# A new written order for the steps of a linear-attention and feed-forward kernel, with the epsilon constants and the bias made early

## The chip, the cores and the metric

The kernel runs on one core of one Trainium2 chip. A core has five engines that work side by side, each through its own list of instructions in order: the matmul engine (PE), the vector engine (DVE), the activation engine (ACT), GpSimd (POOL) and SyncE (SP), which here only issues transfers. Work is handed from one to another by semaphores. The metric is the device time of one execution in microseconds (us); lower is better.

## What is computed

x is 2048 tokens by 448 values, bfloat16. It is normalised, and the output is x + A(xn) + B(xn):

```
xn  = (x - mean) / sqrt(var + 1e-5)
A:  q, k, v = split(xn @ wqkv)              16 heads of 28
    pq, pk  = q @ w_phi, k @ w_phi          per head
    phi     = [softmax(p), softmax(-p)]     56 features
    kv = phi_k^T v,  z = sum_s phi_k
    A  = ((phi_q kv) / (phi_q z + 1e-6)) @ wo
B:  h = xn @ w1 + b1                        1792 features
    B = (h * tanh(softplus(h))) @ w2
```

## The kernel before

The tokens are taken as 16 tiles of 128 (t), in 8 pairs (u). The whole program is a list of named steps. The string ORDER (lines 147 to 161) gives the sequence in which they are recorded, and each engine executes its own instructions in that sequence; each instruction waits only for what it reads or for a place that it overwrites (`Program.op`, L53, and `resolve`, L89). So ORDER decides three things: what each engine does next, in which order SyncE's queue issues the transfers, and which pair of the eight PSUM banks a step gets (`take2`, L391: the pair of banks longest unused).

The steps that the change and the prediction speak of:

- `lx0s` to `lx6s`: loads of x by SyncE (L270); `lx1s` has tiles 2 and 3, `lx2s` 4 and 5, `lx3s` 6 and 7, `lx0s` 0 and 1, `lx4s` 8 to 11, `lx6s` 12 to 15. `lkms lkts lvms` load the weights of k and v, `lqT0` to `lqT3` those of q by transposing transfers (L285), `l1m0s` to `l1m2s` and `l1ts` w1, `l2s` w2, `los` wo, `lbs` the bias (L302), `lpa` w_phi.
- `pi` makes the identity on POOL (L320), `pp pw pm pv pk` other constants; `pk` is mask2 and the zeros of KVT (L349). `ep` is three small instructions on DVE (L362 to L368) that add up columns of the identity into epsT, the epsilon of the denominator. `b1` transposes the bias on PE (L688) and copies it out of PSUM on DVE (`bias_T`, L686).
- `st4d` is the statistics of tile 4 on DVE (L458 and L459), `st5a` the same on ACT (L450 to L454). `rs4p` is 1/sqrt of pair 4 on POOL (L464, L467), `rs4a` and `rs3t` on ACT (L471, L473; `t` tile by tile). `xn4d` normalises pair 4 on DVE in three instructions (L492); `xn7p` does it on POOL (L487), behind a small DVE instruction `sh7` (L480). `xt1d`, `xt1b` transpose the pair on PE and evacuate it on DVE or on both; `xt4m` does it by a transposing transfer of SyncE (L512, called `xTm4` below).
- `wtk0b wmk0b wmq1d bd` and the like fold w_phi into the weights of k and q (L533 to L593); `qd` copies a piece of WqT on DVE. `wmq0`, `wmq1` make Wpq.
- `k1F k1H`, and likewise q and v: pair 1 times the weights, in a part F (three full chunks of 128 rows, six matmuls) and a part H (the last 64 rows, two matmuls side by side); `pair_part` (L418) opens a pair of banks with the first of the two parts and evacuates with the second. `exk`, `exq` are the exponentials on ACT (L614, L675), `ve1` the evacuation of v on ACT or DVE (L507; the letter at the end of the part that comes second says which).
- `kn1.0` sums E of pair 1 (L622) and takes the reciprocal (L624) on DVE, and multiplies on POOL (L626). `kv0` to `kv7` multiply with v on PE (L643), `kvz` masks the sum and adds epsT on DVE (L655), and sends it through a transposing transfer to KVZ.
- `e5` turns the exponentials of q by a transposing transfer (L683, `eT5`). `nd5` is numerator and denominator of tile 5 on PE (L717) and the division on DVE (L732 to L743), `ot2m` turns pair 2 (L752). `f0.3F`, `f0.3H`: chunk 3 of 14 of the feed-forward for half 0 of the tokens on PE, with Mish on ACT (L694). `g5` is the second feed-forward matmul (L818), `wo2F wo2H` the projection (L834); `finish` adds x on DVE (L783). `sto`, `stt` store.

A `kn` step, the place where DVE hands its work to POOL (L622 to L627):

```
        op("DVE", lambda e: e.tensor_reduce(Sk[u][:, s, :], Eh(), AX.X, ALU.add), r=[("E", u, s)], w=[("Sk", u, s)],
           tag=f"Sk{u}.{s}")
        op("DVE", lambda e: e.reciprocal(rSk[u][:, s, :], Sk[u][:, s, :]), r=[("Sk", u, s)], w=[("rSk", u, s)],
           tag=f"rSk{u}.{s}")
        op("POOL", lambda e: e.tensor_tensor(Eh(), Eh(), ap_on(rSk[u][:, s, 0:1], [[1, 2 * H], [0, DH]]), ALU.mult),
           r=[("E", u, s), ("rSk", u, s)], w=[("E", u, s)], tag=f"phik{u}.{s}")
```

Of the kernel before, what the change touches and what calls it, by code (L numbers as in the profile page):

```python
# [144 lines left out]


ORDER = """
lpa lx1s pi lx3s lkms lkts lvms table lx2s st3d pp pw pm lqT1 st6d st2a pv st7d z16 rs3t rs1a xn3d xn1d lqT2 lqT3 lqT0
wtk0b bd xt3b wtk1b xt1d wmk0b st4d v3Fd wmk1d st5a lx6s qd rs2t xn2d lx0s v1Fd v1Ha v3Ha st15d st14d rs7p k1F wmq1d
st12d xn7p wmq0a lx4s st10d xt2m k3F st9d st8d rs4p st11d rs5p st13d k1H l1ts k3H xn4d xt7m q3H q1H q1F l1m2s rs6p q3F  # L150
xn5d xn6p q2F k2F kn3.0 xt4m v2Fd v2Hd xt5m q2H st0d st1d k2H xt6m v7Ha v7Fa rs0p k7F k4F k7H l1m1s e3 xn0d k4H xt0m
v5Hd k6H lbs pk kn1.1 kn3.1 k6F v5Fd kn7.0 kn6.1 k5F k0F k5H e6 kn5.0 v6Ha q4H kn2.0 e2 k0H q4F l1m0s e7 v6Fd ep q6F
v0Fd b1 v0Hd q6H f1.3H f0.0H f1.3F e8 f1.1F f0.0F kn5.1 kn7.1 kn0.1 v4Fa e9 v4Ha kn1.0 f1.0H e13 e12 f1.1H f0.1H kn4.1
kn4.0 f1.0F f0.1F f1.2F los q7H kn6.0 q5H kn0.0 f1.2H q0H e5 e4 kn2.1 q7F q5F q0F f1.13F kv5 kv0 kv7 kv4 kv3 kv6 kv1
kv2 f0.13H f1.13H f0.12H f0.12F f0.13F e0 kvz wob f0.3F e1 f1.8H f0.3H f0.11H l2s nd0 f1.8F f0.11F f1.10F nd1 f1.10H
ot0m e10 e14 e11 f1.9H nd2 f1.9F f1.12F f0.8F f1.12H f0.7H f0.8H nd3 f0.7F f0.2F f1.7F nd5 e15 f1.7H f1.11H f0.2H
f1.11F f0.9F nd4 f1.4H f0.10H f0.9H f1.4F f0.10F ot1m ot2m f0.6F f0.4H f0.5H f0.6H nd12 f0.5F f0.4F f1.5F nd13 f1.6H
ot6m nd8 f1.5H f1.6F g0 g1 wo6F nd7 wo0H nd9 wo6H g12 g13 ot4m wo2F wo0F g5 wo2H nd6 ot3m nd10 nd11 g4 g8 g7 g9 wo3H
ot5m nd15 nd14 wo4H ot7m g6 wo4F g14 g2 g3 g11 wo1F wo7F wo5F wo1H wo5H wo7H sto1 wo3F g10 sto6 sto0 sto5 sto3 sto4
g15 stt14 sto2 stt15  # L160
"""


# [806 lines left out]
```

## Time and profile before

| | us |
|---|---|
| median of 3 runs | 156.01 (155.85 to 156.04) |
| profiled execution | 155.94 |
| its span, first to last instruction | 154.2 |
| PE busy in it | 148.2 |
| DVE, ACT, POOL busy | 103.4, 74.2, 40.9 |

A row of a timeline has the start in us from the span's beginning, the length in us (of a merged group of rows the length from first start to last end), the engine (PE, DVE, ACT, POOL; SPq is SyncE's issue of transfers), the line of the kernel, the operation, what is written from what, the shape (for PE rows*columns of the array, then the moving block), the count, and in brackets the idle time of the engine just ahead of it and what ended that. A row of a table of groups has the same names, then total busy us and mean ns of one, then idle us and releasers. A row of transfers ends with KB each and us from issue to landing.

### The profile page before, as it was taken

To read this page: it belongs to the slowest core of one execution; us is meant where nothing else is said; L and a number is where in the kernel's file an instruction comes from. 1 tells how busy PE (TensorE), PEld (TensorE's weight loads), DVE (VectorE), ACT (ScalarE), POOL (GpSimd) and SP (SyncE) were. 2 spreads that over 40 slices of the span, in tenths; PEclk is the share of its full clock that TensorE was granted. 3 is DMA by queue.
4 is the path that set the end of the run, shared out by engine and by line. 5 is a ranking of instruction groups with operands and counts; after the bars stand their busy time and mean duration, and the time that the engine had idled before them with its cause. 6 is when DMAs were issued, how large, how long until landed. Compare 5 with 4: busy or idle time off the path is not lost.

```text
span 154.2 us, 2908 instructions
## 1 busy us (share of the span) xinstructions
PE 148.2 (96%) x1185; PEld 73.1 (47%) x1185; DVE 103.4 (67%) x228; ACT 74.2 (48%) x94; POOL 40.9 (27%) x58
## 2 busy tenths in 40 slices
PE   7999898999799999999999999999999999999992
PEld 2475343445244457444444444555555555555451
DVE  0897999799999803077978576849759879400641
ACT  3898979889498799676547766100000000000000
POOL 7300679799589991000000000000000000000000
PEclk9999999999999999999999999999999999999999
DMA  5987779998799103994986110300302030300057
GB/s 133 283 135 292 155 154 204 244 173 182 132 168 275 44 6 66 142 286 130 97 169 129 30 34 0 60 4 2 60 0 48 16 60 0 60 4 0 26 194 256
DMA packets 39993, 17.17 MB, mean 111 GB/s; under 512 B 33964, under 2 KB 39212, under 8 KB 39980
## 3 DMA queue, kind: packets, MB, share of 16 engines
q1 hardware_dynamic: 39372, 16.87, 49.4%
q8 instruction: 9, 0.15, 0.4%
q10 hardware_dynamic: 608, 0.12, 0.4%
q14 instruction: 4, 0.03, 0.1%
HBM read 7.02 MB, written 1.84 MB: 57 GB/s over the span
## 4 chain that ended last, share of the span: by engine, by line
PE 71%; DVE 14%; SPq 5%; DMA 3%; POOL 3%; issue 2%; DVEq 0%; POOLq 0%
PE PS L430 32%; PE PS L818 27%; PE PS L834 7%; DVE Sk L622 4%; SPq L285 3%; DVE stats L458 3%; PE PS L717 3%; DMA x_all<-in_A_x_dram 3%; PE PS L643 2%; POOL rstd L467 2%; DVE v_all L507 2%; DVE rSk L624 1%; DVE mv L459 1%; SPq L270 1%; SPq L281 1%
## 5 line engine op out<-in xcount | busy, mean ns | idle before, releaser
L430 PE MATMUL PS<-xnT,W 128*128 128x512 bf16 (+1 forms) x224 | 45.8, 379 | 1.0 <-DVE b1T L507 1.0
L818 PE MATMUL PS<-W,actT 128*128 128x448 bf16 (+1 forms) x224 | 43.2, 351 | 0.0
L694 ACT ACTIVATE actT<-PS,b1T 128x1024 bf16<-128x1024 f32 x28 | 30.8, 1114 | 13.6 <-PE PS L430 13.2
L818 PEld LDWEIGHTS PS<-W,actT 128*128 128x128 bf16 x224 | 21.7, 98 | 20.1 <-issue 0.4
L430 PEld LDWEIGHTS PS<-xnT,W 128*128 128x128 bf16 (+1 forms) x224 | 17.8, 97 | 23.7 <-issue 2.6
L626 POOL TENSOR_TENSOR actT<-actT,rSk 128x896 bf16<-128x896 bf16 x16 | 26.7, 1698 | 3.2 <-DVE rSk L624 3.2
L783 DVE TENSOR_TENSOR x_all<-PS,x_all 128x448 bf16<-128x448 f32 (+1 forms) x16 | 9.2, 614 | 16.8 <-PE PS L834 14.2
L622 DVE TENSOR_REDUCE Sk<-actT 128x32 f32<-128x896 bf16 x16 | 16.6, 1039 | 0.0
L614 ACT ACTIVATE actT<-PS 128x896 bf16<-128x896 f32 x16 | 13.4, 927 | 1.7 <-PE PS L430 1.7
L732 DVE COPY Sq<-PS 128x16 f32<-128x16 f32 x32 | 4.0, 168 | 13.8 <-PE PS L717 13.8
L430 PE MATMUL PS<-Wkv,xnT 128*128 128x448 bf16 (+1 forms) x64 | 12.8, 353 | 0.0
L430 PE MATMUL PS<-Wpk,xnT 128*128 128x448 bf16 (+1 forms) x64 | 12.4, 353 | 0.4 <-DVE v_all L507 0.4
L430 PE MATMUL PS<-Wpq,xnT 128*128 128x448 bf16 (+1 forms) x64 | 12.1, 353 | 0.5 <-DVE Wpq L507 0.5
L458 DVE BATCH_NORM_STATS2 stats<-x_all 128x6 f32<-128x448 bf16 x14 | 8.5, 608 | 4.7 <-DMA x_all<-in_A_x_dram 4.7
L743 DVE TENSOR_TENSOR xn<-v_all,rden 128x448 bf16<-128x448 f32 x16 | 10.0, 625 | 1.8 <-DMA Wkv<-xn 0.7
L740 DVE TENSOR_TENSOR v_all<-v_all 128x464 f32<-128x464 f32 x16 | 10.3, 642 | 0.6
L736 DVE TENSOR_TENSOR v_all<-PS,Sq 128x464 f32<-128x464 f32 x16 | 10.3, 641 | 0.5
L738 DVE TENSOR_TENSOR v_all<-PS,Sq 128x464 f32<-128x464 f32 x16 | 10.1, 631 | 0.0
L675 ACT ACTIVATE actT<-PS 128x896 bf16<-128x896 f32 x10 | 8.6, 933 | 1.0 <-PE PS L430 1.0
L430 PEld LDWEIGHTS PS<-Wpq,xnT 128*128 128x128 bf16 (+1 forms) x64 | 5.1, 97 | 6.6 <-issue 1.1
L430 PEld LDWEIGHTS PS<-Wpk,xnT 128*128 128x128 bf16 (+1 forms) x64 | 5.0, 97 | 6.8 <-issue 1.8
L430 PEld LDWEIGHTS PS<-Wkv,xnT 128*128 128x128 bf16 (+1 forms) x64 | 5.2, 97 | 5.6 <-issue 1.5
(85 smaller groups left out, 122.3 us busy)
## 6 DMA issues: line engine op xcount, KB each, us to landing
W<-in_B_w_dram SPq DMA_DIRECT2D x1, 1568.0 KB, 7.4
out_dram<-x_all SPq DMA_DIRECT2D x7, 224.0 KB, 2.2
W<-in_B_w_dram SPq DMA_DIRECT2D x3, 448.0 KB, 4.1
x_all<-in_A_x_dram SPq DMA_DIRECT2D x4, 224.0 KB, 3.6
x_all<-in_A_x_dram SPq DMA_DIRECT2D x2, 448.0 KB, 4.3
Wkv<-in_A_wqkv_dram SPq DMA_DIRECT2D x2, 336.0 KB, 4.7
Wo<-in_A_wo_dram SPq DMA_DIRECT2D x2, 336.0 KB, 4.3
W<-in_B_w_dram SPq DMA_DIRECT2D x2, 224.0 KB, 3.5
```

What stands on the lines that cost most here:

```text
L430: ins = e.matmul(o, lhs(c, k), rhs(c, k), start=first and c in (0, 3), stop=not first and c in (2, 3))
L458: op("DVE", lambda e: e.bn_stats(stats[:, t, :], x_all[:, t, :]), r=[("x", t)], w=[("st", t)], tag=f"bn{t}")
L614: op("ACT", lambda e, s=s: e.activation(E_of(u)[:, s, :, :], two(b, D), ACT.Exp, scale=1.0 if s == 0 else -1.0), r=[pb(b), pb(b + 1)], w=[ ...
L622: op("DVE", lambda e: e.tensor_reduce(Sk[u][:, s, :], Eh(), AX.X, ALU.add), r=[("E", u, s)], w=[("Sk", u, s)], tag=f"Sk{u}.{s}")
L626: op("POOL", lambda e: e.tensor_tensor(Eh(), Eh(), ap_on(rSk[u][:, s, 0:1], [[1, 2 * H], [0, DH]]), ALU.mult), r=[("E", u, s), ("rSk", u, ...
L694: op("ACT", lambda e: e.activation(actT[:, fc, q * 1024:(q + 1) * 1024], bank(b, 2), ACT.Mish, bias=b1T[:, fc:fc + 1]), r=[("b1T",), pb(b) ...
L736: op("DVE", lambda e: e.tensor_tensor(tv(t1[i]), num(0), sx(1), ALU.mult), r=[pb(b), pb(b + 1), ("Sq", i, 1)], w=[("t1", i)], tag=f"ta{t}")
L738: op("DVE", lambda e: e.tensor_tensor(tv(t2), num(1), sx(0), ALU.mult), r=[pb(b), pb(b + 1), ("Sq", i, 0)], w=[("t2",)], tag=f"tb{t}")
L740: op("DVE", lambda e: e.tensor_tensor(t1[i], t1[i], t2, ALU.add), r=[("t1", i), ("t2",)], w=[("t1", i)], tag=f"tc{t}")
L743: op("DVE", lambda e: e.tensor_tensor(o_sb[(t // 2) % 2][:, t % 2, :].rearrange("p (h d) -> p h d", d=DH), t1[i][:, :, 0:DH], ap_on(rden[i ...
L818: ins = e.matmul(bank(b)[:, 0:width(t)], actT[:, fc, tok(t)], W2[:, fc, 0:width(t)], start=first and fc == 0, stop=last and fc == FC - 1)
L834: ins = e.matmul(bank(b)[:, 0:n], oT_of(u)[lo:hi, cc * P:(cc + 1) * P], Wo[lo:hi, cc, 0:n], start=first and c in (0, 3), stop=last and c i ...
```

## The change

It replaces the string ORDER by another with the same 290 steps in a new sequence. Fifteen of them go to another engine or form. `ep` comes third, behind `pp` and `pi`, and so is the first work of DVE; before, it stood in the middle. `lbs` comes behind `lvms` in SyncE's queue, and `b1` ahead of `v3Fa` on PE; before, `lbs` stood behind `xt0m`, and `b1` behind the matmuls of v0F. `lqT2` now stands ahead of `lx2s`. `pk` is made at the start instead of behind `rs0p`. The other forms: `rs0` from POOL to ACT, `rs3` from ACT to POOL, `rs4 rs5` from POOL to ACT, `st5` from ACT to DVE, `xt1` from DVE alone to both, `wmk1` from DVE to ACT, `wmq0` from ACT to DVE and `wmq1` from DVE to ACT, and the evacuation of v4 from ACT to DVE and of v0 from DVE to ACT (of v1, v3, v6 and v7 only the letter of the part that comes first changes, which evacuates nothing). No function changes.

```diff
@@ -145,19 +145,19 @@
 
 
 ORDER = """
-lpa lx1s pi lx3s lkms lkts lvms table lx2s st3d pp pw pm lqT1 st6d st2a pv st7d z16 rs3t rs1a xn3d xn1d lqT2 lqT3 lqT0
-wtk0b bd xt3b wtk1b xt1d wmk0b st4d v3Fd wmk1d st5a lx6s qd rs2t xn2d lx0s v1Fd v1Ha v3Ha st15d st14d rs7p k1F wmq1d
-st12d xn7p wmq0a lx4s st10d xt2m k3F st9d st8d rs4p st11d rs5p st13d k1H l1ts k3H xn4d xt7m q3H q1H q1F l1m2s rs6p q3F
-xn5d xn6p q2F k2F kn3.0 xt4m v2Fd v2Hd xt5m q2H st0d st1d k2H xt6m v7Ha v7Fa rs0p k7F k4F k7H l1m1s e3 xn0d k4H xt0m
-v5Hd k6H lbs pk kn1.1 kn3.1 k6F v5Fd kn7.0 kn6.1 k5F k0F k5H e6 kn5.0 v6Ha q4H kn2.0 e2 k0H q4F l1m0s e7 v6Fd ep q6F
-v0Fd b1 v0Hd q6H f1.3H f0.0H f1.3F e8 f1.1F f0.0F kn5.1 kn7.1 kn0.1 v4Fa e9 v4Ha kn1.0 f1.0H e13 e12 f1.1H f0.1H kn4.1
-kn4.0 f1.0F f0.1F f1.2F los q7H kn6.0 q5H kn0.0 f1.2H q0H e5 e4 kn2.1 q7F q5F q0F f1.13F kv5 kv0 kv7 kv4 kv3 kv6 kv1
-kv2 f0.13H f1.13H f0.12H f0.12F f0.13F e0 kvz wob f0.3F e1 f1.8H f0.3H f0.11H l2s nd0 f1.8F f0.11F f1.10F nd1 f1.10H
-ot0m e10 e14 e11 f1.9H nd2 f1.9F f1.12F f0.8F f1.12H f0.7H f0.8H nd3 f0.7F f0.2F f1.7F nd5 e15 f1.7H f1.11H f0.2H
-f1.11F f0.9F nd4 f1.4H f0.10H f0.9H f1.4F f0.10F ot1m ot2m f0.6F f0.4H f0.5H f0.6H nd12 f0.5F f0.4F f1.5F nd13 f1.6H
-ot6m nd8 f1.5H f1.6F g0 g1 wo6F nd7 wo0H nd9 wo6H g12 g13 ot4m wo2F wo0F g5 wo2H nd6 ot3m nd10 nd11 g4 g8 g7 g9 wo3H
-ot5m nd15 nd14 wo4H ot7m g6 wo4F g14 g2 g3 g11 wo1F wo7F wo5F wo1H wo5H wo7H sto1 wo3F g10 sto6 sto0 sto5 sto3 sto4
-g15 stt14 sto2 stt15
+pp pi ep lpa pk lx1s st3d table lx3s st2a lkms z16 pw pm st6d lkts lvms st7d rs1a lbs lqT2 lx2s rs3p pv xn1d xn3d
+wtk0b bd xt1b wtk1b xt3b wmk0b st5d wmk1a st4d v1Fa v1Ha rs2t lqT1 k3H v3Ha lqT3 lqT0 qd lx6s b1 xn2d lx0s lx4s v3Fa
+wmq1a xt2m st14d wmq0d st15d l1m2s k3F rs7p l1m1s st12d xn7p k1F q1H k1H q1F q3F k2F st9d st8d v2Hd st13d rs4a xt7m
+k2H e2 rs6p xn4d xn6p q2H q3H st11d st0d st10d v2Fd kn1.1 q2F k7F xt4m st1d rs5a v7Fd xn5d xt6m kn2.1 e7 v4Ha rs0t e3
+q4H v7Ha xn0d k7H v4Fd kn2.0 q4F k4F q6F e6 kn7.1 kn3.0 xt5m xt0m l1m0s v6Hd q6H k4H k6H v6Fd kn7.0 e13 k6F k0F k5F
+v0Hd e12 l1ts k5H kn4.1 kn1.0 k0H kn6.0 v5Hd v0Fa v5Fd q0F f1.1F q0H kn3.1 f1.1H f0.2H e5 f1.0H f1.0F kn0.1 kn6.1
+kn5.1 los f0.2F f0.3F f0.1F e8 e9 e1 f0.1H q5H f0.3H e4 q7H kn5.0 q5F q7F f0.11F kv5 kv6 kv7 kn0.0 kn4.0 kv2 e0 kv3
+kv1 kv0 kv4 e11 e14 f0.11H f1.2H kvz f0.8H f0.8F f1.2F e15 f1.11F f0.6F nd2 f0.6H f1.11H f0.9H f0.9F f0.12F nd0 f1.12H
+f0.12H e10 nd1 f1.12F f0.7F f1.7F f1.7H f1.10H f0.7H nd3 f1.10F ot0m l2s f1.3F f1.13F nd5 f1.13H f0.5H f1.3H f0.5F
+f1.4F ot1m nd4 f0.13H f1.4H nd6 f0.13F f1.6F f0.4F f1.6H f0.10H f0.4H nd7 f0.10F f1.8F ot3m f0.0F nd10 f1.8H f0.0H
+f1.5H f1.5F ot2m f1.9F wo1F nd13 f1.9H nd11 wo1H g2 g7 g3 g1 wo3F ot5m wo3H nd12 wo0H nd14 g6 wo0F wo2F g0 g5 ot6m nd8
+nd9 wo2H nd15 g4 g11 wo5F g8 sto2 ot7m ot4m g13 g9 g12 sto1 g10 wo7F wo6F wo4F wob wo5H wo7H wo6H wo4H sto3 sto5 g14
+sto6 g15 sto4 stt14 sto0 stt15
 """
```

## Prediction

> **What bounds the kernel now.** I read the page's shares first, then the timeline of the matmul engine for the places where it waits, then the timelines of the engines it waits for, then the issues of SyncE.
>
> ```profile
> span 154.2 us, 2908 instructions
> ...
> PE 148.2 (96%) x1185; PEld 73.1 (47%) x1185; DVE 103.4 (67%) x228; ACT 74.2 (48%) x94; POOL 40.9 (27%) x58
> ...
> 16.46 4.06 PE L430 MATMUL PS<-Wpq,xnT 64*128 64x448 bf16 x22 [0.54 <-DVE Wpq L507]
> 25.31 2.93 PE L430 MATMUL PS<-Wpk,xnT 128*128 128x448 bf16 x16 [0.41 <-DVE v_all L507]
> 40.69 4.38 PE L430 MATMUL PS<-xnT,W 64*128 64x512 bf16 x20 [1.03 <-DVE b1T L507]
> 56.77 3.33 PE L643 MATMUL PS<-actT,v_all 128*60 128x112 bf16 x128
> 60.03 5.57 PE L430 MATMUL PS<-xnT,W 64*128 64x512 bf16 x30
> ```
>
> PE is busy for 148.2 of 154.2 us; between its warm-up and the output it waits at three places: 0.54 + 0.41 + 1.03 = 1.98 us. The change alters the order of PE's work and hardly its amount, so about 2 us can be won at most, and new waits can cost more. Behind kv (L643, 56.77 to 60.03) PE never waits, so the two orders are told apart in the first 60 us.
>
> **The wait of 1.03 us.**
>
> ```profile
> 38.89 1.66 DVE L367 SCALAR_TENSOR_TENSOR epsT<-epsT 128x1 f32<-128x1 f32 x1
> ...
> 38.84 1.70 POOL L626 TENSOR_TENSOR actT<-actT,rSk 128x896 bf16<-128x896 bf16 x1
> ```
>
> One element took DVE 1.66 us: L367 starts 0.05 us behind a product of 1.70 us on POOL and ends with it (40.55 against 40.54). The reductions, reciprocals and PSUM reads of DVE run beside such products at their usual length, so it is this kind of instruction that waits for POOL. The bias stands behind it on DVE, and a bank that PE wants behind the bias. With `ep` first on DVE and `b1` early, this pair stands between PE and no bank: 1.03 us go. `ep` itself now runs when the identity is made, on POOL behind the three memsets of `pp`, while DVE otherwise waits for the first x; it costs nothing.
>
> **The start, to 16 us.**
>
> ```profile
> 4.07 0.48 SPq L270 DMA_DIRECT2D x_all<-in_A_x_dram  x1
> 4.59 5.11 SPq L285 DMA_TRANSPOSE WqT<-in_A_wqkv_dram  x4
> 9.74 1.53 SPq L270 DMA_DIRECT2D x_all<-in_A_x_dram  x3
> ...
> 30.06 0.61 SPq L302 DMA_DIRECT2D b_rows<-in_B_b_dram  x1
> ...
> x_all<-in_A_x_dram SPq DMA_DIRECT2D x1, 448.0 KB, 4.0
> ...
> 13.79 0.63 DVE L458 BATCH_NORM_STATS2 stats<-x_all 128x6 f32<-128x448 bf16 x1 [1.00 <-DMA x_all<-in_A_x_dram]
> 15.28 1.12 DVE L507 CAST Wpq<-PS 128x448 bf16<-128x448 f32 x2
> ```
>
> `lbs` (0.61) now goes ahead of `lx2s`, all of `lqT` and `lx6s lx0s lx4s`. `lx6s` is issued at 9.74 + 0.61 = 10.35 and lands 4.0 later, at 14.4 (before: 13.75, and DVE waited for it). `lx2s` falls behind one of the transposes as well (1.28 by pitch), to about 6.0; DVE has until 14.4 for its two tiles. DVE then takes one tile's statistics (0.73, below), not two, between that landing and the evacuation of Wpq: 14.4 + 0.73 + 1.12 = 16.25. PE's `q1H` starts at 16.3, where `q3H` started at 16.46; PE has done `b1` more and `k1H` (0.18) less. So the 0.54 us wait stays, in effect: I take 0. POOL now makes `pk`, `vare3`, `rstd3` and `pv` ahead of `bd`, so Wbd and `wmk0b` come some 0.5 us later; that lies inside the same wait of PE, and would cost its 0.5 without it.
>
> **DVE from 14.4 to the first `kn`.**
>
> ```profile
> 18.59 0.59 DVE L458 BATCH_NORM_STATS2 stats<-x_all 128x6 f32<-128x448 bf16 x1
> ...
> 19.32 0.59 DVE L458 BATCH_NORM_STATS2 stats<-x_all 128x6 f32<-128x448 bf16 x1
> ...
> 28.68 1.07 DVE L622 TENSOR_REDUCE Sk<-actT 128x32 f32<-128x896 bf16 x1
> 29.79 0.35 DVE L624 RECIPROCAL rSk<-Sk 128x32 f32<-128x32 f32 x1
> ...
> 37.70 1.03 DVE L507 CAST v_all<-PS 128x896 bf16<-128x896 f32 x1
> ...
> 19.80 0.71 POOL L467 TENSOR_TENSOR rstd<-lnv,mhalf 128x2 f32<-128x2 f32 x1
> ```
>
> A tile's statistics have a pitch of 0.73. Nine of them make 6.57; `wmq0d` 1.05, `sh7` with its wait for POOL's rstd7 (0.71) 0.5, `xn4d` 0.9, `sh6` 0.15, `ve2` 0.95, `Sk1.1` and `rSk1.1` 1.45: 14.4 + 11.6 = 26.0, say 26.1. Before, `xn5d` came ahead of every `kn`, and `xn0d` when POOL had no product in hand. Now `xn5d` follows `kn1.1` with one tile's statistics between, and `xn0d` follows `kn2.1` directly. Each `kn` leaves 1.70 us of product on POOL. Whether xn's L492 waits for a product as L367 did, the trace shows over no product. From both sides: nothing, or the rest of the product, for each. The nearest rows:
>
> ```profile
> 21.26 0.37 DVE L492 TENSOR_SCALAR xn<-x_all,mv,rstd 128x384 bf16<-128x384 bf16 x1
> 21.71 0.63 DVE L492 TENSOR_SCALAR xn<-x_all,mv,rstd 128x448 bf16<-128x448 bf16 x2
> 21.47 0.25 POOL L464 TENSOR_SCALAR lnv<-mv 128x2 f32<-128x2 f32 x1
> ...
> L492 DVE TENSOR_SCALAR xn<-x_all,mv,rstd 128x448 bf16<-128x448 bf16 x6 | 2.3, 388 | 1.2 <-POOL rstd L467 1.1
> ...
> L492 DVE TENSOR_SCALAR xn<-x_all,mv,rstd 128x64 bf16<-128x64 bf16 x6 | 1.8, 296 | 0.3 <-ACT rstd L473 0.3
> ```
>
> On DVE an instruction starts about 0.08 before the last one's record ends, so the one at 21.71 was due at 21.55; it starts as POOL's short one ends (21.72). POOL got in between two such instructions, and DVE waited. Also, 384 more elements cost L492 92 ns, about 4 per ns, where L622 takes 1.07 us for 896: it is another kind of access than the reduction's. So I take the upper end. The Trainium skill, page "SBUF — State Buffer", section "Who interferes with whom", says that GpSimd and VectorE share a pair of ports as an exclusive lock held for a whole instruction, and that a VectorE instruction needs it when it has two SBUF inputs or runs in a two-port mode, which `tensor_scalar` can. L367 (two SBUF inputs, 1.66 us) agrees, and by that rule L492 waits too: 157.0 as forecast; if only two-input instructions waited, it would be the second rival's 155.0.
>
> With the waits: the product of `kn1.1` runs from 26.2 to 27.9. `xn5d`, due at 26.8, waits 1.1 and ends at 28.8; `kn2.1` is through DVE at 30.2. The first of `xn0d`'s three instructions is ahead of POOL (0.39), then POOL's waiting product goes, 30.5 to 32.2, and the other two end at 32.8, 1.7 late. `ve4` behind them ends at 33.8. Without the waits it would end at 31.0.
>
> **PE in the same stretch.**
>
> ```profile
> 20.36 1.30 PE L430 MATMUL PS<-Wpk,xnT 128*128 128x448 bf16 x6
> 21.49 1.59 PE L430 MATMUL PS<-Wkv,xnT 128*128 128x448 bf16 x8
> 22.92 0.35 PE L430 MATMUL PS<-Wpq,xnT 64*128 64x448 bf16 x2
> ...
> 65.76 4.06 PE L430 MATMUL PS<-xnT,W 128*128 128x512 bf16 x18
> ...
> 70.73 4.81 PE L430 MATMUL PS<-xnT,W 128*128 128x512 bf16 x24
> ...
> 17.30 1.74 POOL L487 TENSOR_SCALAR xn<-x_all,rstd,shift 128x448 bf16<-128x448 bf16 x3 [0.83 <-DVE shift L480]
> ...
> 26.52 0.95 ACT L505 ACTIVATE v_all<-PS 128x896 bf16<-128x896 f32 x1
> ...
> xnT<-xn SPq DMA_TRANSPOSE x1, 3.3
> ```
>
> From start to start an F part of q, k or v takes 1.13 to 1.14, F with H 1.43, an H alone 0.18 to 0.19 (0.35 with the pipeline's tail): so 0.1 for each change to H. Of the feed-forward, three F take 4.06, 1.35 each, and three F with three H 4.81, 0.25 for an H. From 16.3 these bring PE to `k7F` at 23.4; `xTm7` is issued at about 20.0, behind POOL's `xn7p` (1.74, from `sh7` at 18.2), and lands at 23.3 to 23.8 (two W1 loads now go before it). `k4F` needs the banks of v7: ACT's `ln0` waits for `st1d` on DVE (26.9), then `ve7` (0.95) ends at 28.4. Three F later, at 31.9, `v6H` takes the banks that held v4 and needs `ve4`: 33.9. So PE stands for 2.0 us. From `v6H` to `kv5` lie nine F at 1.14, eleven H at 0.19, six F at 1.35, five H at 0.25 and five changes: 22.2; the same rates fall about 0.5% short of the stretch from 16.46 to 56.77, its waits taken out, so 22.3. `kv5` starts at 56.2, and after kv's 3.26 the next step at 59.45.
>
> POOL does not set a later time:
>
> ```profile
> 43.09 14.95 POOL L626 TENSOR_TENSOR actT<-actT,rSk 128x896 bf16<-128x896 bf16 x9 [2.55 <-DVE rSk L624]
> ```
>
> That is 1.66 each; the fourteen products behind `rSk2.0` (35.2) end at 58.5, and `kv4`, the last eighth of kv, at 58.9.
>
> **The sum.** Before, kv ended at 60.03 with one more feed-forward step done (1.35 + 0.25): 58.45 for the same work. Now 59.45: +1.0 us. The waits of 1.98 become 0.5 at `q1H`, some 0.5 to 1 around `k7F` and `k4F`, and 2.0 at `v6H`. Behind kv the order costs nothing as long as `nd2` finds KVZ:
>
> ```profile
> 60.15 1.38 DVE L655 SCALAR_TENSOR_TENSOR KVT<-PS,epsT,mask 60x448 bf16<-60x448 f32 x2 [6.48 <-PE PS L643]
> ...
> KVZ<-KVT SPq DMA_TRANSPOSE x1, 3.2
> EqT<-Eq SPq DMA_TRANSPOSE x1, 4.7
> ```
>
> KVZ lands 1.5 + 3.2 = 4.7 behind kv, at 64.2, under four F and three H of feed-forward (6.2 us, to 65.6); with the longest flight of a transpose seen (4.7) it would land at 65.7, so this cover is 1.4 us thick and each further us would count. The profiled execution took 155.94 (1.74 around its span), 0.07 below the median of 156.01; on the median's scale the forecast is 157.0, with its own range 156.3 to 157.7 from the landing of `lx6s`, which moves DVE and PE alike (0.6 either way).
>
> **Rivals.**
> - DVE keeps its turn through all of `xn0d`, and POOL's product waits 0.9 instead. For: DVE is ahead by some 0.2 us. Against: POOL got in at 21.72. `ve4` ends at 32.1, 0.2 after `v6H` is due, and kv ends at 57.7: 155.25. Chance 0.18.
> - L492 doesn't wait for POOL, only the two-input L367 does. `ve4` (31.0) is in time, kv ends at 57.45: 1.0 us faster, 155.0. Chance 0.14.
> - All three waits go and none comes: 154.0. Against: `lx6s` is issued later, not earlier. Chance 0.05.
> - The late DVE of the forecast drags SyncE's queue: `xTm0`, behind `xn0d` (32.8), lands with a flight of 4.7 at 37.6, 0.5 after `k0F` is due, and W1's tail, issued behind `eT13 eT12` and so behind q6's exponentials, is late by as much again in front of `f1.1F`. It decides from a flight of 4.2 us on; 157.6, or 158.2 with `lx6s` late too. Chance 0.13.
>
> **How the numbers follow.** The forecast has 0.5. A measurement of this kernel tells 0.2% (0.3 us) from no change. Slower: the forecast and the last rival but for the forecast's lowest edge, 0.60. Faster: the first three rivals but for an edge of the first, 0.33. Within 0.2%: 0.07. The range goes from 154.9, just below the second rival, to 158.2.
>
> **What would show it.** L492 records of over 1 us at about 27 and 30, ending with a product of POOL; a wait of PE of about 2 us between 32 and 34, put down to DVE's v_all L507; L367 at 0.2 us or less before the first statistics; no wait of PE for b1T; kv from about 56 on. It is wrong if L492 keeps 0.3 to 0.4 us beside a product, if PE's wait for v4's banks is under 0.8 us, or if PE waits behind kv.

## The result, and the profile after

| | median us | lowest to highest | runs | ratio to before, 95% |
|---|---|---|---|---|
| before | 155.97 | 155.85 to 156.04 | 4 | |
| after | 157.12 | 156.81 to 157.42 | 4 | 1.0074 (1.0049 to 1.0099) |

The new order is 1.15 us slower. The profiled execution of after took 156.91 us, that of before 155.94. These are the page's first lines and then the matmul engine's timeline of after, the rows that answer to those of before:

```profile
span 154.6 us, 2902 instructions
...
PE 148.8 (96%) x1185; PEld 73.8 (48%) x1185; DVE 104.7 (68%) x229; ACT 73.8 (48%) x95; POOL 38.8 (25%) x54
```

```profile
16.51 0.36 PE L430 MATMUL PS<-Wpq,xnT 64*128 64x448 bf16 x2
...
26.38 0.36 PE L430 MATMUL PS<-Wkv,xnT 64*128 64x448 bf16 x2 [0.30 <-DMA xnT<-xn]
...
33.38 0.36 PE L430 MATMUL PS<-Wkv,xnT 64*128 64x448 bf16 x2 [1.42 <-DVE v_all L507]
...
43.72 1.46 PE L430 MATMUL PS<-xnT,W 128*128 128x512 bf16 x6 [0.39 <-ACT v_all L505]
...
55.92 3.34 PE L643 MATMUL PS<-actT,v_all 128*60 128x112 bf16 x128
59.19 6.11 PE L430 MATMUL PS<-xnT,W 64*128 64x512 bf16 x30
65.52 0.40 PE L717 MATMUL PS<-KVZ,EqT 56*128 56x60 bf16 x16 [0.22 <-DMA KVZ<-KVT]
```

The three waits of before (0.54, 0.41, 1.03; 1.98 us) are gone, and four others have come: 0.30 at `v4H` for pair 4's transposed xn, 1.42 at `v6H` for the evacuation of v4, 0.39 at `f1.1F`, 0.22 for KVZ; 2.33 us. The step behind kv starts at 59.19; the same work was done at 58.45 before, so kv is 0.74 late. The arithmetic closes if the start is counted in: before, PE had work up to 15.92 and then waited 0.54; in after it is busy up to 16.51 with hardly more work, 0.59 late. 0.59 + 0.30 + 1.42 + 0.39 - 1.98 = 0.72. These terms don't stand for themselves, though: `v6H` starts when DVE has evacuated v4, so a PE that came there earlier would only wait longer (in `a_dma` below the 0.30 is gone, and the wait at `v6H` is 1.72). With KVZ's 0.22 the last group of matmuls is 0.95 late, as the two timelines show, first before, then after:

```profile
150.61 0.57 PE L800 MATMUL PS<-W,actT 128*128 128x64 bf16 x14
```

```profile
151.56 0.57 PE L800 MATMUL PS<-W,actT 128*128 128x64 bf16 x14
```

The spans differ by only 0.4 us, because the last store landed in 1.7 us in after's profile and in 2.3 in before's; the time outside the span was 2.3 against 1.7. For a comparison the last matmul or the whole time is the better mark.

Where the 1.42 comes from shows in DVE's and POOL's timelines of after (the rows at 30.14, 30.35 and 31.95 are the parts of one group, `xn0d`, in time order):

```profile
27.05 1.79 DVE L492 TENSOR_SCALAR xn<-x_all,mv,rstd 128x448 bf16<-128x448 bf16 x3
...
30.14 0.30 DVE L492 TENSOR_SCALAR xn<-x_all,mv,rstd 128x448 bf16<-128x448 bf16 x1
30.35 1.68 DVE L492 TENSOR_SCALAR xn<-x_all,mv,rstd 128x64 bf16<-128x64 bf16 x1
31.95 0.37 DVE L492 TENSOR_SCALAR xn<-x_all,mv,rstd 128x384 bf16<-128x384 bf16 x1
32.24 1.08 DVE L507 CAST v_all<-PS 128x896 bf16<-128x896 f32 x1
```

```profile
26.51 1.70 POOL L626 TENSOR_TENSOR actT<-actT,rSk 128x896 bf16<-128x896 bf16 x1 [2.80 <-DVE rSk L624]
30.30 1.70 POOL L626 TENSOR_TENSOR actT<-actT,rSk 128x896 bf16<-128x896 bf16 x1 [2.09 <-DVE rSk L624]
```

Three L492 take some 0.9 us alone. `xn5d` took 1.79, `xn0d` 2.18, so they lost 0.9 and 1.3. In `xn5d` the first of the three has a record of 1.29 us, to 28.34, where POOL's product ended at 28.21. In `xn0d` the first instruction gets through, POOL's product starts at 30.30, and the second, 64 elements wide, has a record of 1.68 us that ends with the product (32.03 against 32.00). That is a wait, though the profile's page counts it as busy. `ve4` ends at 33.32, and `v6H` starts 0.06 later.

The two small steps, in DVE's timeline of after:

```profile
2.77 0.16 DVE L367 SCALAR_TENSOR_TENSOR epsT<-epsT 128x1 f32<-128x1 f32 x1
...
12.39 0.17 DVE L507 CAST b1T<-PS 128x14 f32<-128x14 bf16 x1
13.27 0.93 DVE L492 TENSOR_SCALAR xn<-x_all,mv,rstd 128x448 bf16<-128x448 bf16 x3 [0.71 <-ACT rstd L473]
```

L367 is 0.16 instead of 1.66 us, and no wait for b1T is left. The third row is used below.

### The profile page after: what moved, and what is told of

It reads as the page before. It is cut to its first block, busy times and chain, and to the rows that moved or that the text cites. A ratio compares the mean times of both kernels' runs of the same rounds, so it can differ in the third digit from the quotient of the medians.

```text
span 154.6 us, 2902 instructions
## 1 busy us (share of the span) xinstructions
PE 148.8 (96%) x1185; PEld 73.8 (48%) x1185; DVE 104.7 (68%) x229; ACT 73.8 (48%) x95; POOL 38.8 (25%) x54
## 4 chain that ended last, share of the span: by engine, by line
PE 78%; ACT 7%; DMA 6%; DVE 6%; issue 1%; POOL 1%; SPq 0%
PE PS L430 37%; PE PS L818 27%; PE PS L834 7%; ACT actT L614 4%; DMA KVZ<-KVT 3%; PE PS L717 3%; DVE xn L492 2%; PE PS L643 2%; DMA x_all<-in_A_x_dram 2%; DMA EqT<-actT 1%; PE PS L576 1%; DVE stats L458 1%; ACT actT L675 1%; ACT Eq L675 1%; DVE KVT L655 1%
## 5 line engine op out<-in xcount | busy, mean ns | idle before, releaser
L694 ACT ACTIVATE actT<-PS,b1T 128x1024 bf16<-128x1024 f32 x28 | 29.8, 1112 | 15.1 <-PE PS L430 10.0
L430 PE MATMUL PS<-Wpq,xnT 128*128 128x448 bf16 (+1 forms) x64 | 12.7, 353 | 0.0
L458 DVE BATCH_NORM_STATS2 stats<-x_all 128x6 f32<-128x448 bf16 x15 | 9.0, 603 | 0.8 <-DMA x_all<-in_A_x_dram 0.8
L492 DVE TENSOR_SCALAR xn<-x_all,mv,rstd 128x448 bf16<-128x448 bf16 (+2 forms) x18 | 8.2, 511 | 1.5 <-ACT rstd L473 1.2
```

The costliest lines, as they stand in the source:

```text
L430: ins = e.matmul(o, lhs(c, k), rhs(c, k), start=first and c in (0, 3), stop=not first and c in (2, 3))
L458: op("DVE", lambda e: e.bn_stats(stats[:, t, :], x_all[:, t, :]), r=[("x", t)], w=[("st", t)], tag=f"bn{t}")
L492: op("DVE", lambda e, t=t, lo=lo, hi=hi, at=at: e.tensor_scalar(X[:, at:at + hi - lo], x_all[:, t, lo:hi], mv[:, t, 0:1], rstd[:, t:t + 1] ...
L694: op("ACT", lambda e: e.activation(actT[:, fc, q * 1024:(q + 1) * 1024], bank(b, 2), ACT.Mish, bias=b1T[:, fc:fc + 1]), r=[("b1T",), pb(b) ...
```

## The experiments

Each but `a_probe` is the kernel before or the kernel after with some names moved in ORDER; a diff shows the stretches of names that change. Times are medians, with the ratio to the kernel before on the same chip.

### Only the epsilon early (`b_ep`), on the kernel before

```diff
-pi lx3s
+pi ep lx3s
...
-v6Fd ep q6F
+v6Fd q6F
```

> The order of before with one step moved: ep straight behind pi. Theory (the wait of 1.03 us was DVE's L367 waiting for POOL's product, the bias merely stood behind it): L367 takes 0.2 us or less near 2 us, b1T's evacuation comes 1.5 us earlier, PE's wait for it goes, 155.97 - 1.0 to 1.2 = 154.8 to 155.0. Rival (PE waited for the bias, which came late): no gain, 155.9 to 156.1.

Measured: 155.04 us (154.4 to 155.46), ratio 0.9938 (0.9919 to 0.9957). DVE's and PE's timelines:

```profile
2.03 0.16 DVE L367 SCALAR_TENSOR_TENSOR epsT<-epsT 128x1 f32<-128x1 f32 x1
...
13.60 0.63 DVE L458 BATCH_NORM_STATS2 stats<-x_all 128x6 f32<-128x448 bf16 x1 [0.63 <-DMA x_all<-in_A_x_dram]
```

```profile
16.26 4.06 PE L430 MATMUL PS<-Wpq,xnT 64*128 64x448 bf16 x22 [0.17 <-DVE Wpq L507]
24.96 3.00 PE L430 MATMUL PS<-Wpk,xnT 128*128 128x448 bf16 x16 [0.26 <-DVE v_all L507]
32.14 1.59 PE L430 MATMUL PS<-Wpk,xnT 128*128 128x448 bf16 x8 [0.29 <-DMA xnT<-xn]
```

No wait for b1T remains although the bias stands where it stood. The wait of 1.03 was L367 alone, and moving one step of three small instructions is worth 0.96. The bias only stood behind it. (PE's other waits changed too, from 0.54 and 0.41 to 0.17, 0.26 and a new 0.29, so the 0.96 is not this one term by itself.)

### Only the bias early (`b_b1`), and both early (`b_ep_b1`), on the kernel before

```diff
-lvms table
+lvms lbs table
...
-v3Ha st15d
+v3Ha b1 st15d
...
-k6H lbs pk
+k6H pk
...
-v0Fd b1 v0Hd
+v0Fd v0Hd
```

`b_ep_b1` has the edit of `b_ep` as well.

> The order of before with the bias alone made early: lbs behind lvms, b1 behind v3Ha; ep stays where it was. Theory: L367 keeps its 1.66 us, and the next that stands behind it, v0's evacuation, ends at about 41.6 and holds PE at f1.1F for some 0.5 us instead of 1.03; lbs ahead of lx6s makes DVE's wait for x 0.6 us longer: the two cancel, 155.8 to 156.3. Rival (the bias was late): the 1.03 us go, 154.9 or with the later x 155.5.

> The order of before with both ep and the bias made early, as in the change. Theory (lbs ahead of x's last loads makes them land 0.6 us later, and DVE, which waits for them, hands that on in part; the bias early brings nothing by itself): 0.2 to 0.6 us slower than with ep alone, 155.2 to 155.6. Rival (both help): 154.6 to 155.0.

Measured: `b_b1` 155.64 us (155.42 to 155.92), ratio 0.9978 (0.9967 to 0.9989); `b_ep_b1` 155.77 (155.38 to 156.24), ratio 0.9988 (0.9975 to 1.0002). The timelines, first of `b_b1`:

```profile
39.45 1.66 DVE L367 SCALAR_TENSOR_TENSOR epsT<-epsT 128x1 f32<-128x1 f32 x1
...
42.17 2.76 PE L430 MATMUL PS<-xnT,W 128*128 128x512 bf16 x12 [0.41 <-DVE v_all L507]
```

and of `b_ep_b1`:

```profile
14.12 0.63 DVE L458 BATCH_NORM_STATS2 stats<-x_all 128x6 f32<-128x448 bf16 x1 [1.08 <-DMA x_all<-in_A_x_dram]
...
16.80 4.06 PE L430 MATMUL PS<-Wpq,xnT 64*128 64x448 bf16 x22 [0.65 <-DVE Wpq L507]
26.05 2.93 PE L430 MATMUL PS<-Wpk,xnT 128*128 128x448 bf16 x16 [0.81 <-DVE v_all L507]
```

With the bias out of its way L367 still waits 1.66 us, and PE stands for the next thing in DVE's list, the evacuation of v0. And beside an early `ep` the early bias costs 0.73 us (155.77 against 155.04): its 0.6 us in SyncE's queue brings `lx6s` 0.52 later (14.12 against 13.60), and PE's start at Wpq is 0.54 later. In this order DVE waits for that very load. Both medians fell a little outside what was expected: 155.64 is 0.16 below its range, 155.77 is 0.17 above.

### Which DVE instructions wait for POOL (`a_probe`), on the kernel after

Six DVE instructions on places that nothing else reads, recorded behind the last `kn` while POOL still has three products in hand. The computation of the kernel is unchanged; the instructions are extra work. This kernel ran once, in 157.26 us.

```diff
+op("DVE", lambda e: e.tensor_reduce(F0[:, 0:1], ap_on(ident[:, DH:DH + 1], [[64, 2], [DH + 2, 2]]), AX.XY, ALU.add),
...
+op("DVE", lambda e: e.tensor_scalar(X1[:, :], x_all[:, 1, :], mv[:, 2, 0:1], rstd[:, 2:3],
...
+op("DVE", lambda e: e.reciprocal(F1[:, :], rSk[4][:, 0, :]), r=r, w=[("pr", 2)], tag="pr2")
+op("DVE", lambda e: e.tensor_tensor(F2[:, 0:2], mv[:, 2, :], mv[:, 3, :], ALU.add), r=r, w=[("pr", 3)], tag="pr3")
+op("DVE", lambda e: e.bn_stats(F3[:, :], x_all[:, 1, :]), r=r, w=[("pr", 4)], tag="pr4")
+op("DVE", lambda e: e.tensor_scalar(X2[:, 0:64], x_all[:, 1, 0:64], mv[:, 2, 0:1], rstd[:, 2:3],
```

> The changed kernel with six more instructions on DVE behind the last kn, while POOL has six products in a row and DVE has 5 us of idle time; they write scratch tiles and change no result. In order: a tensor_reduce with one SBUF input, a tensor_scalar of 448 bf16 as in xn, a reciprocal of 32, a tensor_tensor of two SBUF inputs with 2 elements, a bn_stats of 448, a tensor_scalar of 64 bf16. Theory (two SBUF inputs, and the tensor_scalar, wait for the running product; the others do not): the second, fourth and sixth each last until a product of POOL ends, up to 1.7 us, the first, third and fifth keep 0.15, 0.35 and 0.6 us. Rival (only two SBUF inputs wait): only the fourth is long. Time within 0.5 us of the changed kernel.

DVE's timeline of that stretch, and POOL's:

```profile
53.96 0.10 DVE L374 TENSOR_REDUCE pf<-ident 128x1 f32<-128x4 bf16 x1
54.08 0.80 DVE L376 TENSOR_SCALAR pr<-x_all,mv,rstd 128x448 bf16<-128x448 bf16 x1
54.81 0.34 DVE L378 RECIPROCAL pf<-rSk 128x32 f32<-128x32 f32 x1
55.07 1.39 DVE L379 TENSOR_TENSOR pf<-mv 128x2 f32<-128x2 f32 x1
56.38 0.61 DVE L380 BATCH_NORM_STATS2 pf<-x_all 128x6 f32<-128x448 bf16 x1
56.92 1.31 DVE L381 TENSOR_SCALAR pr<-x_all,mv,rstd 128x64 bf16<-128x64 bf16 x1
```

```profile
53.05 1.70 POOL L640 TENSOR_TENSOR actT<-actT,rSk 128x896 bf16<-128x896 bf16 x1
54.71 1.73 POOL L640 TENSOR_TENSOR actT<-actT,rSk 128x896 bf16<-128x896 bf16 x1
56.40 1.69 POOL L640 TENSOR_TENSOR actT<-actT,rSk 128x896 bf16<-128x896 bf16 x1
```

The products end at 54.75, 56.44 and 58.09. The reduction, the reciprocal and the statistics keep their usual length. Both `tensor_scalar` and the `tensor_tensor` on two elements last until just behind the product that runs (54.88, 56.46, 58.23). So it isn't the count of large inputs: `tensor_scalar` has one, and 64 elements suffice. The Trainium skill, page "SBUF — State Buffer", section "Who interferes with whom", says that two SBUF inputs contend with a GpSimd instruction that reads SBUF, that `tensor_scalar` can enter a two-port mode that contends with GpSimd, that the later of the two blocks for the whole of the other's instruction, and that `tensor_reduce` never contends on trn2. The four records of these operations agree with it; the reciprocal and the statistics it doesn't name. That a two-port mode is what makes `tensor_scalar` wait is not shown here: this form also reads two scalars per partition from SBUF, and no run tells the two apart.

### The two `kn` steps away from `xn` (`a_kn`), on the kernel after

```diff
-v2Fd kn1.1 q2F
+v2Fd q2F
...
-xt6m kn2.1 e7
+xt6m e7
...
-xn0d k7H v4Fd kn2.0
+xn0d kn1.1 k7H v4Fd kn2.1 kn2.0
```

> The changed kernel with two steps moved: kn1.1 behind xn0d, kn2.1 behind v4Fd; nothing else. Theory (the loss is xn5d and xn0d waiting on DVE for POOL's products): all L492 records at 0.3 to 0.4 us, v4's evacuation ends near 30.6, PE's wait of 1.42 us before v6H goes, and POOL's last product ends near 57: 157.1 - 1.4 = 155.5 to 155.9. Rival (the new order is late for other reasons, the kn only fill the time): 156.9 to 157.3.

Measured: 155.6 us (155.15 to 156.62), ratio 0.9978 (0.996 to 0.9996). The profiled execution is the slowest of these, 156.62:

```profile
26.61 1.70 DVE L492 TENSOR_SCALAR xn<-x_all,mv,rstd 128x448 bf16<-128x448 bf16 x6 [0.46 <-ACT rstd L473]
...
43.75 1.46 PE L430 MATMUL PS<-xnT,W 128*128 128x512 bf16 x6 [1.52 <-DMA W<-in_B_w_dram]
```

All six L492 now take 1.70 together, PE doesn't wait at `v6H`, and the kernel is 1.5 us faster than after.

The move takes more away than the two waits: `kn2.1`'s own sum and reciprocal, 1.4 us, no longer stand in front of v4's evacuation either. What each would do alone can be estimated from after's rows, as DVE has no gap from 24.96 to 33.32 there. PE is due at `v6H` at 31.96 (33.38 - 1.42). Without the two waits the evacuation of v4 would end near 31.1 (33.32 - 0.9 - 1.3), without `kn2.1`'s work near 31.9, so either is about enough. No run takes the waits away and leaves the work.

In this execution PE reached `f1.1F` earlier and met the next late thing there, the last columns of W1 (`l1ts`), which stand in SyncE's queue behind two transposes of q's exponentials. After's 0.39 at the same step, which its row puts down to ACT's evacuation of v0, is the same transfer: two loads issued from 39.11, the second some 0.6 later, with a flight (from issue to landing) of 3.8 land at about 43.5. `a_probe`, which is the kernel after up to its six instructions at 54 us, has 0.93 there, and its row names the transfer:

```profile
44.31 1.46 PE L444 MATMUL PS<-xnT,W 128*128 128x512 bf16 x6 [0.93 <-DMA W<-in_B_w_dram]
```

So the size of this wait differs from one execution to the next. The next run takes it away.

### Only two transfers moved (`a_dma`), on the kernel after

```diff
-xt0m l1m0s v6Hd
+xt0m l1m0s l1ts v6Hd
...
-e12 l1ts k5H
+e12 k5H
...
-kv4 e11 e14 f0.11H f1.2H kvz f0.8H
+kv4 f0.11H f1.2H kvz e11 e14 f0.8H
```

> The changed kernel with the transfers alone moved: l1ts straight behind l1m0s, e11 e14 behind kvz; kn1.1 and kn2.1 stay. Theory: PE keeps its 1.4 us before v6H; the waits at f1.1F (0.39) and for KVZ (0.22) go: 156.4 to 156.8. Rival (0.39 and 0.22 are covered by other waits): 157.1.

Measured: 156.06 us (155.96 to 156.39), ratio 1.0005 (0.9995 to 1.0015). The only wait of PE from 10 us on, then the start of `f1.1F`, and ACT's evacuation of v0:

```profile
33.47 0.36 PE L430 MATMUL PS<-Wkv,xnT 64*128 64x448 bf16 x2 [1.72 <-DVE v_all L507]
...
43.26 1.46 PE L430 MATMUL PS<-xnT,W 128*128 128x512 bf16 x6
```

```profile
42.77 0.95 ACT L505 ACTIVATE v_all<-PS 128x896 bf16<-128x896 f32 x1
```

The waits at `f1.1F` and for KVZ are gone, and `f1.1F` starts at 43.26 while ACT is still evacuating v0 (42.77 to 43.72): it never needed that. `v6H` starts when it did in after (33.47 against 33.38), with PE there earlier and waiting longer.

That the wait for KVZ is gone isn't shown to come from the edit. `a_probe` leaves `e11 e14` ahead of KVZ as after does, and its transfer rows are:

```profile
57.55 3.21 SPq L697 DMA_TRANSPOSE EqT<-actT  x2
61.31 1.23 SPq L675 DMA_TRANSPOSE KVZ<-KVT  x1
...
KVZ<-KVT SPq DMA_TRANSPOSE x1, 3.2
```

There KVZ lands in 3.2 us, in `a_kn` with the same queue in 3.3, where after has 4.7; with `e11 e14` behind it, it took 3.2 in `a_dma`, `a_all` and `a_late`, but 4.2 in `a_kn2` and 4.4 in `a_best`. In none of these does PE wait for it. What makes this flight long stays open.

The gain is 1.06, more than the 0.61 of the two waits in after's profile and outside what was expected (156.4 to 156.8); the last matmuls end 0.74 earlier. After's profiled execution was 0.21 below its median, and the wait for W1's tail can be larger than its 0.39 (0.93 above), which may be the rest; no profile of after shows it.

### Both (`a_all`), and only `kn2.1` with the transfers (`a_kn2`)

`a_all` has the edits of `a_kn` and `a_dma`; `a_kn2` the same but for `kn1.1`, which stays ahead of `xn5d`.

> The kernel with kn1.1 and kn2.1 moved, and besides l1ts straight behind l1m0s and e11 e14 behind kvz in SyncE's queue. Theory (with DVE's wait for POOL gone, the next thing late is W1's tail, held in SyncE's queue by eT13 and eT12: PE waited 1.52 us for it in that run's profile): the wait at f1.1F goes, KVZ flies 3.2 to 4.0 us instead of 4.7: 154.8 to 155.2. Rival (PE's arrival at kv is set by POOL's products or ACT by then): no better than 155.6.

> The kernel after with W1's tail and the EqT transposes moved as in a_dma, and kn2.1 behind v4Fd; kn1.1 stays ahead of xn5d. My theory: xn5d still waits some 0.9 us for the product of kn1.1, xn0d waits for none, so v4's evacuation ends about 2.3 us minus the 1.4 us of kn2.1's sum and reciprocal earlier, near 30.6 to 31.2, in front of the time at which v6H is due (31.9): one wait of 0.9 is hidden, v6H doesn't wait, 154.9 to 155.2. Rival: every microsecond that DVE waits shows on PE, and then about half of the gain of moving both (1.1) stays out: 155.4 to 155.7.

Measured: `a_all` **154.94 us** (154.89 to 154.98), ratio 0.9932 (0.992 to 0.9945); `a_kn2` 155.04 (155.02 to 155.08), ratio 0.9936 (0.992 to 0.9953). DVE's and POOL's timelines of `a_kn2`:

```profile
27.12 2.59 DVE L492 TENSOR_SCALAR xn<-x_all,mv,rstd 128x448 bf16<-128x448 bf16 x6
29.64 1.08 DVE L507 CAST v_all<-PS 128x896 bf16<-128x896 f32 x1
```

```profile
26.59 1.70 POOL L626 TENSOR_TENSOR actT<-actT,rSk 128x896 bf16<-128x896 bf16 x1 [2.81 <-DVE rSk L624]
```

The six L492 take 2.59 against 1.70: `xn5d` does wait 0.9 for `kn1.1`'s product. It costs nothing in this order. `ve4` (v4's evacuation) ends at 30.72, and PE takes its banks at 31.65, with no wait. In after the same 0.9 stands in front of `ve4` together with `xn0d`'s 1.3 and `kn2.1`'s own 1.4, and `ve4` ends at 33.32; there it is not free, as without it alone `ve4` would end near 32.4, still behind 31.96 (an estimate from after's rows).

What PE waits for next is POOL: 0.28 us ahead of the last eighth of kv in `a_all`, 0.17 ahead of kv and 0.28 ahead of its last eighth in `a_kn2`.

### Is the early bias worth keeping? (`a_best`, `a_late`), on `a_all`

`a_best` puts `lbs` behind `lx4s` and `b1` behind `q2H`; `a_late` puts them where the kernel before had them.

```diff
-rs1a lbs lqT2
+rs1a lqT2
...
-lx6s b1 xn2d
+lx6s xn2d
...
-xt0m l1m0s
+xt0m lbs l1m0s
...
-v0Hd e12
+v0Hd b1 e12
```

> The kernel with kn1.1, kn2.1, l1ts, e11 and e14 moved, and lbs behind lx4s with b1 behind q2H, so that lx6s is issued 0.6 us earlier. Theory: 0.2 to 0.6 us faster than without the last move, 154.3 to 154.9. Rival (the wait for x's late tiles is hidden by PE's other work): as without it.

> The kernel of a_all with the bias load behind xt0m and its transposition behind v0Hd, where the kernel before had them. Theory A: the early bias costs 0.6 us of SyncE's queue, and lx6s, now earlier, lets DVE reach Wpq earlier: 154.3 to 154.7. Theory B: in this order DVE waits at 13.35 for ACT's rstd of pair 2 and not for lx6s, so the earlier load is worth nothing there: 154.8 to 155.1, and PE's q1H starts at 16.3 to 16.6 as in a_all. The turn of b1 in the banks can cost up to 0.4 more where it stands.

Measured: `a_best` 156.16 us (156.02 to 157.96), ratio 1.0035 (1.0005 to 1.0066), slower where a gain was expected; `a_late` **154.74** (154.57 to 154.81), ratio 0.9915 (0.9899 to 0.993). PE of `a_best`:

```profile
22.85 0.18 PE L688 MATMUL PS<-ident,b_rows 14*128 14x14 bf16 x1 [1.64 <-ACT actT L614]
```

The one small matmul of the bias fell on a pair of banks that ACT was still reading for k's exponentials; PE stood 1.64 us, so the time says nothing about the queue. (Three of its twelve executions took 157.9, the others 156.0 to 156.3.) `a_late`, on DVE and PE:

```profile
13.23 0.94 DVE L492 TENSOR_SCALAR xn<-x_all,mv,rstd 128x448 bf16<-128x448 bf16 x3 [0.97 <-ACT rstd L473]
```

```profile
16.36 0.36 PE L430 MATMUL PS<-Wpq,xnT 64*128 64x448 bf16 x2
```

PE's `q1H` comes at 16.36 against 16.59 in `a_all`, with `lx6s` and its two neighbours issued 0.56 earlier. DVE waits for ACT's rstd of pair 2 just ahead, at 13.23 against 13.35: in these two profiles the load of the last tiles isn't what DVE waits for, and the early bias costs 0.2 there at most, with its matmul on PE. `a_best`, with the same early `lx6s`, has the same wait to 13.35, and `q1H` at 16.48. But the early bias leaves little room: in `a_kn`'s profile the load landed later, and DVE did wait for it,

```profile
14.63 0.63 DVE L458 BATCH_NORM_STATS2 stats<-x_all 128x6 f32<-128x448 bf16 x1 [0.32 <-DMA x_all<-in_A_x_dram]
```

where `a_all` had these statistics at 14.19. PE's `q1H` came at 16.61 all the same. The medians of `a_late` and `a_all` differ by 0.2, and the intervals of their ratios overlap.

## Why the prediction was right, step by step

The time (157.0 forecast, 157.12 measured) and its main cause were right: DVE's waits for POOL hold v4's evacuation and with it PE at `v6H`. That the time is only 0.12 off is in part luck: several sizes were off, and they cancelled. From `v6H` on, against the sum: it starts 0.5 early (33.38 against 33.9), the stretch to kv is 0.15 shorter without its wait (22.15 against 22.3), and the two waits of 0.39 and 0.22 that the sum lacked come on top.

- **The wait of 1.03 goes since L367 waited for POOL.** Shown by `b_ep` (155.04 against 156.00) and `b_b1`, where L367 stays and the wait moves on to v0's evacuation.
- **`lx6s` lands 0.6 later and the 0.54 us wait stays.** PE's `q1H` came at 16.51 (forecast 16.3), but not for that reason. After's DVE waited for ACT's rstd ahead of `xn2d` (0.71, at 13.27) and its next statistics name no wait for x; in `a_kn` they do (0.32). `a_late` puts the early bias at 0.2 at most in the new order; the 0.6 would have been right in the old one, as `b_ep_b1` shows (0.73). PE was busy up to 16.51 in after's profile, as its warm-up group lasted 6.57 us, 0.90 longer than in before's; in the other runs of this order, with a shorter warm-up, it waited 0.23 to 0.81 for xn at about 8.8 and came out at the same 16.4 to 16.6.
- **DVE reaches the end of `rSk1.1` at 26.1.** 26.42 (26.07 + 0.35).
- **Both `xn` steps wait for POOL, 1.1 and 1.7; `ve4` ends at 33.8.** The kind was right, also that POOL gets its turn behind the first instruction of `xn0d`. The sizes were 0.9 and 1.3. The products ended 1.16 and 1.65 us after the instructions were due, close to the forecast, but the sum put the waiting instruction's own time behind the product, and its record ends with it (28.34 against 28.21, 32.03 against 32.00), as L367's did before. `ve4` ended at 33.32. `a_probe` shows the kind over six instructions; `a_kn` and `a_kn2` show the effect, together with that of `kn2.1`'s own work.
- **POOL got in between two L492 at 21.72 in before.** This reading is not safe. The instruction at 21.71 is the first of `xn5d`, which needs pair 5's rstd, and POOL finished that at 21.68:

```profile
20.80 0.88 POOL L467 TENSOR_TENSOR rstd<-lnv,mhalf 128x2 f32<-128x2 f32 x1
```

That explains the start without any turn of POOL's. The choice that rested on it came true: in after POOL's product starts at 30.30.
- **PE waits 0.5 to 1 at `k7F` and `k4F`, and 2.0 at `v6H`.** No wait came at the first two but 0.30 at `v4H`. v7's banks held nothing: their evacuation ended at 28.50, and PE came to `k4F` at 29.52. From there to `v6H` lie two F and not three, so that the 31.9 for `v6H` was met (31.96) is luck. `v6H` waited 1.42. Since the end of `ve4` sets its start, the waits in front of it cost nothing.
- **kv at 56.2, the step behind it at 59.45.** 55.92 and 59.19, by a sum that lacks the 0.39 for W1's tail in front of `f1.1F`. The prediction had this only inside its last rival, tied to a flight above 4.2; it came at 3.8 (0.93 in `a_probe`, 1.52 in `a_kn`).
- **POOL's last product at 58.5.** 58.03, not on the path.
- **Behind kv nothing, as long as KVZ is in time.** It wasn't: with the flight of 4.7 that the prediction gave as the upper end it cost 0.22, against 0.1 reckoned. A wait of PE behind kv was one of the prediction's own signs of being wrong; it concerns this term, and in no other profile of the new order does PE wait for KVZ. The transfer rows of after:

```profile
56.95 3.24 SPq L683 DMA_TRANSPOSE EqT<-actT  x2
60.71 1.23 SPq L661 DMA_TRANSPOSE KVZ<-KVT  x1
...
KVZ<-KVT SPq DMA_TRANSPOSE x1, 4.7
```

`eT11` and `eT14` go out just ahead of KVZ, but `a_probe` and `a_kn` with the same queue have 3.2 and 3.3, so they are not shown to be the reason.

Of the rivals, "DVE keeps its turn through `xn0d`" falls on the row at 30.30, and "only the two-input L367 waits" on `a_probe`. "All waits go" falls on the same rows. The last rival's W1 half came about, in small, its `xTm0` half not. Moving what these rows name gives kernels that beat both: `a_all`, 154.94, and `a_late`, 154.74, about 1.3 us under the kernel before and 2.4 under the kernel after. What the move of `e11 e14` adds to that is not shown.

## What to carry to other kernels

Where DVE hands work to POOL, DVE's next instruction decides: put reductions, statistics or PSUM reads behind the hand-over and keep `tensor_scalar` and two-input operations clear of it, but only where what hangs on them has no slack. A record that is many times the usual length of its instruction (1.68 us for 0.30 here) can be a wait, though the profile counts it as busy; look at what ends when it ends. When one wait is taken away, ask the timeline for the transfer that the next step needs: here it was W1's last columns, 1.52 us behind PE in `a_kn`, most of which the earlier wait had hidden. And before a queue is blamed for a late transfer, look at the same transfer in every profile: KVZ's was late once, and the same queue was on time twice.

## What the runs showed of the hardware

- One element on DVE can cost a whole product of POOL: 0.16 against 1.66 us for L367, and 0.30 against 1.68 for 64 elements of L492. The record ends with the product, 0.01 to 0.14 us behind it. POOL in turn gets in between two such instructions of DVE that follow each other directly (30.30, between those at 30.14 and 30.35).
- The flight of one transposing transfer, KVZ's, was 3.2 or 3.3 us in nine profiles and 4.2, 4.4 and 4.7 in three, with and without two others just ahead of it in the queue. The cause is open.
- PE's warm-up group of the same 16 matmuls took from 5.44 to 6.57 us over these profiles. In the new order that changes nothing: PE then waits for xn instead, and `q1H` starts at 16.36 to 16.61 in all eight profiles.
- The time of the whole execution beyond the span was 1.74 to 2.00 us in the four profiles of the old order, where the last store landed in 2.3, and 2.07 to 2.36 in the eight of the new, where it landed in 1.7. So a comparison of spans alone makes the new order look better than it is.
